# Padded bin rows, and one plain loop in place of staggered stages, in a Fourier filter with routed experts

## The chip, the core and the metric

The kernel runs on one core of one Trainium2 chip. The metric is device time in microseconds, the median of several runs. The engines are called PE (TensorE), DVE (VectorE), ACT (ScalarE), POOL (GpSimd) and SP (SyncE); PE, DVE, ACT and POOL compute, and SP only issues DMAs here.

## The reference

What is computed, cut to what matters (B = 8 batches, S = 2496 positions, D = 256 columns, N = B S = 19968 rows, E = 8 experts of hidden size 1024):

```python
X = np.fft.rfft(x, axis=1)
Y = X * (filt_r + 1j * filt_i)[None]
y = np.fft.irfft(Y, n=S, axis=1).reshape(N, D)

logits = y @ w_gate + modality_bias[modality_id]
e_idx = np.argmax(logits, axis=1)
gate_w = softmax(logits)[arange(N), e_idx]
for e in range(E):
    mask = e_idx == e
    h = np.maximum(y[mask] @ w1[e], 0.0)
    out[mask] = gate_w[mask, None] * (h @ w2[e])
```

## The kernel before

The Fourier transform of length 2496 = 48 x 52 is done as products with small matrices, in three stages per batch, all in 16-bit floats with sums in PSUM.

- **Stage one** (`stage1`, 13 pieces a batch): products of `w1m` with pieces of x (L222); ACT copies each piece to `t1` (L225), and SP writes every second one to the DRAM buffer `b1_d` (L228).
- **Stage two** (`stage2`, 12 pieces and one step behind): `t2` is read back from `b1_d` in three chunks (L415); products with `w2m` (L431), ACT copies to `xf` (L443), DVE multiplies with the filters `g1` and `g2` (L445, L446), products with `a1m` and `a2m` (L438, L439), ACT copies to `z` (L452), and SP writes to `b2_d` (L454).
- **Stage three** (`stage3`, 10 pieces and two steps behind): `t4` is read from `b2_d` in four chunks (L422); products with `wbm` (L477, L478), scaled into `yo` by ACT or DVE by turns; a step later the rows are transposed on PE (L489) and copied to `yT` by DVE (L498); another step later they are multiplied with the gate weights (L494), and DVE adds the logits (L507).
- **Routing** (`count`, `place`, `table`): the expert of each row, its place in the expert's bin, and the blocks of 256 rows that are full. `scatter` writes the rows of `yo` to the bins in DRAM with indirect DMAs from POOL (L561). A row of a bin holds 256 halves, the row's number and its gate weight: RW = 130 words, 520 bytes.
- **Experts** (`Experts.step`): a block of a bin is loaded by SP (L635), turned by PE (L661), multiplied with the first matrix (L672), passed through relu by ACT (L676), multiplied with the second (L684), scaled by DVE (L691) and scattered to the output by POOL (L694). There are 85 blocks, four steps each. Up to three blocks are loaded ahead.

The tiles of `t2` and `t4` come from one pool of three buffers (`bp`, tag `t24`), and the PSUM tiles of the three stages, of the transposes `lt` and of `place` from another of three (`pp`, tag `ps`). A new tile waits until the one three allocations earlier has been read.

Ahead of the loop the matrices are made: POOL writes index patterns, DVE makes phases of them, ACT takes the sine (`turns_to_cos`, L190). Stage one of batch 0 is written between `w1m` and the larger `w2m`. `a1m` and `a2m` are `w2m` and a changed copy `w2x` of it, turned by products with a permutation (L309), evicted by DVE and ACT. Half of each filter tile is read from DRAM, and the other half is copied within SBUF (L258, L259).

One loop then runs over steps n. Batch g is offset by `GAP` = 14 steps from the batch before it; its stage two starts at 14 g + 16 and its stage three at 14 g + 32; `load_t2` and `load_t4` are asked `LEAD` = 2 steps ahead; `count` comes 12 steps after the start of stage three and `place` one later. Each step also runs 2.25 expert steps (`STEPS`), and the weights of one expert are asked on every fourth step from the first on. What is left of the experts follows the loop. The framework orders the instructions of each engine from this program: an engine works through its own instructions in order, and so do the DMA queues of SP and POOL.

Of the kernel before, what the change touches and what calls it, by code (L numbers as in the profile page):

```python
# [20 lines left out]
P = 128  # L21
# [7 lines left out]
def kernel(  # L29
# [47 lines left out]
    RW = DW + 2  # L77
# [11 lines left out]

    RND = float(3 << 22)  # L90
    TWO_PI = 2.0 * math.pi

    zbias = const_pool.tile([P, 1], F32)
    nc.vector.memset(zbias, 0.0)
# [20 lines left out]

# [13 lines left out]
    pp = ctx.enter_context(tc.tile_pool(name="fpsum", bufs=3, space=bass.MemoryType.PSUM))  # L129
    hp = ctx.enter_context(tc.tile_pool(name="hpsum", bufs=2, space=bass.MemoryType.PSUM))  # L130
    op = ctx.enter_context(tc.tile_pool(name="opsum", bufs=1, space=bass.MemoryType.PSUM))
# [18 lines left out]
    gen = tc.alloc_tile_pool(name="gen", bufs=1)  # L150
    k1_i = gen.tile([KA, 2, NS], I, name="k1_i")
    nc.gpsimd.iota(k1_i, pattern=[[0, 2], [1, NS]], base=0, channel_multiplier=0)
    for _ in range(3):
        load_x()
    k2_i = gen.tile([KB, NS, N2], I, name="k2_i")
    nc.gpsimd.iota(k2_i, pattern=[[1, NS], [N1, N2]], base=0, channel_multiplier=0)
    nc.gpsimd.iota(k2_i[:, :, H:N2], pattern=[[1, NS], [-N1, H]], base=N1 * (N2 - 1), channel_multiplier=0)
    nc.gpsimd.iota(k2_i[:, 0, :], pattern=[[N1 // 2, 2], [N1, H]], base=0, channel_multiplier=0)


    wg_f = const_pool.tile([P, DC, E], F32)
    nc.sync.dma_start(wg_f, moe_w_gate.rearrange("(a p) e -> p a e", p=P))
    mb_sb = const_pool.tile([1, n_mod * E], F32)
    nc.sync.dma_start(mb_sb, moe_modality_bias.rearrange("a e -> (a e)")[None, :])
    mid_h = dataclasses.replace(moe_modality_id.tensor, shape=list(moe_modality_id.tensor.shape))
    mid32 = mid_h.ap().bitcast(I32).rearrange("(g p w) -> p g w", g=B, p=KA)
    mraw = gen.tile([P, B, 2 * NTT], I32, name="mraw")
    nc.sync.dma_start(mraw[:KA], mid32)
    mrawc = gen.tile([P, 3, B, 2 * NTT], I32, name="mrawc")
    for b in range(3):  # L170
        nc.sync.dma_start(mrawc[KA:P, b], mid32[b * KC:(b + 1) * KC])
    rows = row_int([], rows_i, "rows")
    bit0 = row_int([(ALU.bitwise_and, 1)], rows_i, "bit0")
    half = row_int([(ALU.arith_shift_right, 1)], rows_i, "half")
    def col(name, fn):
        t = fft_pool.tile([P, 1], F32, name=name)
        fn(t)
        return t
# [5 lines left out]
    nbit0 = col("nbit0", lambda t: ts(t, bit0, -1.0, 1.0))  # L184
    def turns_to_cos(dst, q, shape):

        r = gen.tile(shape, F32, tag="gen_r")
        ts(r, q, RND, RND, ALU.add, ALU.subtract)
        nc.vector.tensor_sub(q, q, r)
        nc.scalar.activation(dst, q, AF.Sin, bias=zbias[:shape[0], :], scale=TWO_PI)  # L190


    k1_f = gen.tile([KA, 2, NS], F32, name="k1_f")
# [13 lines left out]
    NP = NTT // EV  # L207
    NPY = NY // EV
    st = [dict() for _ in range(B)]

    def chunk_of(t):
        for c, (t0, t1) in enumerate(TCH):
            if t0 <= t < t1:
                return c, t0, t1

    def stage1(g, k):
        t = k * EV
        c, t0, t1 = chunk_of(t)
        xt = xts[g, c]
        ps = pp.tile([P, EV, D], F32, tag="ps")  # L220
        for i in range(EV):
            nc.tensor.matmul(ps[:KA, i, :], lhsT=w1m, rhs=xt[:, t - t0 + i, :], start=True, stop=True)  # L222
        if k % 2 == 0:
            st[g]["t1"] = rp.tile([KA, 2, EV, D], BF16, tag="t1", bufs=2, name="t1")
        nc.scalar.copy(st[g]["t1"][:, k % 2], ps[:KA])  # L225
        if k % 2 == 1 or k == NP - 1:
            n = (k % 2 + 1) * EV
            nc.sync.dma_start(b1_d[g, t + EV - n:t + EV].rearrange("t p c -> p t c"),  # L228
                              st[g]["t1"].rearrange("p a b d -> p (a b) d")[:, :n])

    def input_piece(g, k):

        stage1(g, k)
        if (k + 1) * EV in [t1 for t0, t1 in TCH]:
            load_x()

    ident = const_pool.tile([P, P], BF16)
    make_identity(nc, ident)

    Lexcl = const_pool.tile([P, P], F32)  # L240
    nc.gpsimd.memset(Lexcl, 0.0)
    nc.gpsimd.affine_select(
        out=Lexcl, in_=Lexcl, compare_op=ALU.is_ge, fill=1.0,
        base=0, pattern=[[-1, P]], channel_multiplier=1,
    )
    ones_sq = const_pool.tile([P, P], F32)
    nc.vector.memset(ones_sq, 1.0)


    for f_dram, g in ((filt_r, g1), (filt_i, g2)):  # L250
        by_c = f_dram[0:N1 * H, :].rearrange("(c s) d -> c s d", s=N1)
        rev = bass.AP(f_dram.tensor, f_dram.offset + (N1 - 1) * D,
                      [[N1 * D, H], [-D, NS - 1], [1, D]])
        nc.gpsimd.dma_start(g[0:H, 0:NS, :], by_c[:, 0:NS, :])
        nc.gpsimd.dma_start(g[H:N2, 1:NS, :], rev)
        nc.gpsimd.dma_start(g[H:N2, 0, :], by_c[:, NS, :])
        nc.gpsimd.dma_start(g[N2:N2 + 1, 0, :], f_dram[NF - 1:NF, :])
        nc.sync.dma_start(g[N2:KB, 1:NS, :], g[0:N2, 1:NS, :])  # L258
        nc.sync.dma_start(g[N2 + 1:KB, 0, :], g[1:N2, 0, :])  # L259

    for k in range(NP):
        input_piece(0, k)

    bit1 = row_int([(ALU.arith_shift_right, 1), (ALU.bitwise_and, 1)], rows_i, "bit1")
    quart = row_int([(ALU.arith_shift_right, 2)], rows_i, "quart")


    x_ro = col("x_ro", lambda t: nc.vector.tensor_single_scalar(t, rows, float(N2), op=ALU.is_ge))
    x_c = fft_pool.tile([P, 1], F32, name="x_c")
    nc.vector.scalar_tensor_tensor(x_c, in0=x_ro, scalar=-float(N2), in1=rows, op0=ALU.mult, op1=ALU.add)  # L270
    x_hi = col("x_hi", lambda t: nc.vector.tensor_single_scalar(t, x_c, float(H), op=ALU.is_ge))
    sgn = col("sgn", lambda t: ts(t, x_hi, -2.0, 1.0))
    x_c0 = col("x_c0", lambda t: nc.vector.tensor_single_scalar(t, x_c, 0.0, op=ALU.is_equal))
    wt0 = col("wt0", lambda t: ts(t, x_c0, -0.5, 1.0))

# [5 lines left out]
    ph1 = col("ph1", lambda t: ts(t, bit0, -0.25, 0.5))  # L281
    q2 = gen.tile([KB, NS, 2, N2], F32, name="q2")
    ts(q2[:, :, 0, :], k2_i, n2s[:KB], ph0[:KB])
    ts(q2[:, :, 1, :], k2_i, n2s[:KB], ph1[:KB])

    ts(q2[:, 0, 0, :], k2_i[:, 0, :], n2s[:KB], 0.25)
    ts(q2[:, 0, 1, :], k2_i[:, 0, :], n2s[:KB], 0.5)
# [6 lines left out]


# [9 lines left out]
    for s0 in range(0, NS, SPB):  # L305
        for src, dst in ((w2m, a1m), (w2x, a2m)):
            tp = pp.tile([P, EV * D], F32, tag="ps", name="tp")
            for i in range(SPB):
                nc.tensor.matmul(tp[:KB, i * KB:(i + 1) * KB], lhsT=src[:, s0 + i, :], rhs=perm,  # L309
                                 start=True, stop=True)  # L310
# [467 lines left out]
    while True:  # L778
# [3 lines left out]
        for g in range(B):  # L782
# [3 lines left out]
            if 0 <= k <= NS // EV:  # L786
                stage2(g, k)
# [63 lines left out]
```

## Time and profile before

| | |
|---|---|
| time, median of 3 runs | 876.86 us (872.82 to 879.74) |
| the profiled execution | 879.74 us |
| its span | 878.0 us |
| its mean granted PE clock | 0.811 |
| PE busy | 650.8 us (74%) |
| DVE, ACT, POOL busy | 385.7, 387.3, 367.7 us (44%, 44%, 42%) |
| DMA bytes | 106.80 MB |

The page gives the busy time of each engine, and the span in 40 slices of 22 us with the granted PE clock and the share of time that the 16 DMA engines were busy. Windows give the same for any stretch. A timeline lists instructions with their start, duration and, in brackets, the idle time of the engine ahead of them and what ended it. Starts of products on PE are times of issue, and their ends are modelled.

### The profile page before, as it was taken

The numbers are of one execution on the slowest core, as the hardware profiler recorded it, in microseconds if no ns is written. First come the engines' busy times: TensorE is split into PE (matmuls) and PEld (weight loads), VectorE is DVE, ScalarE is ACT, GpSimd is POOL, SyncE is SP. The second block draws the span as 40 slices with busy tenths as digits, with TensorE's granted clock in tenths as the row PEclk, the third lists the DMA queues.
The fourth block names the chain that finished last, engine by engine and source line by source line (L and its number), as shares of the span: only waits on it lengthen the run. The fifth ranks groups of instructions, "written<-read, shape, count | busy, mean of one in ns | idle before, by whom it ended". The sixth has DMA issues, their size and how long they took to land.

```text
span 878.0 us, 15948 instructions
## 1 busy us (share of the span) xinstructions
PE 650.8 (74%) x4886; PEld 497.7 (57%) x4886; DVE 385.7 (44%) x1248; ACT 387.3 (44%) x695; POOL 367.7 (42%) x413
## 2 busy tenths in 40 slices
PE   1463678697596787787956886877694679999996
PEld 1352446465365556565744674665473457777775
DVE  5431235346255434553733464454253224444442
ACT  1553335345254444463724543452242235555553
POOL 5131201625505433544345345435546544444444
PEclk9985555557579878897969899897897769999998
DMA  8799986566465446454533343342222223222320
GB/s 154 162 223 211 225 176 159 130 139 173 105 149 149 121 100 160 119 149 100 168 110 112 100 115 117 88 127 71 70 73 95 95 79 101 94 92 92 96 64 1
DMA packets 92696, 106.80 MB, mean 122 GB/s; under 512 B 12708, under 2 KB 75754, under 8 KB 92460
## 3 DMA queue, kind: packets, MB, share of 16 engines
q0 software_dynamic: 29120, 50.75, 24.8%
q1 hardware_dynamic: 63496, 55.03, 23.9%
q8 instruction: 44, 0.72, 0.4%
q14 instruction: 36, 0.29, 0.1%
HBM read 71.87 MB, written 54.31 MB: 144 GB/s over the span
## 4 chain that ended last, share of the span: by engine, by line
PE 23%; issue 17%; POOL 8%; another core or an unknown queue 4%; DMA 4%; DVE 3%; ACT 2%; POOLq 0%; SPq 0%; DVEq 0%; ACTq 0%
PE hps L672 7%; PE ops L684 6%; POOL out_dram L694 6%; DMA out_dram<-osb,meta 2%; PE ps L478 2%; POOL bins_d L561 2%; PE ps L477 2%; PE lt L489 1%; DMA bins_d<-yo,pos_i 1%; ACT hT L676 1%; PE ps L431 1%; PE pT L661 1%; PE pz L439 1%; PE pz L438 1%
## 5 line engine op out<-in xcount | busy, mean ns | idle before, releaser
L676 ACT ACTIVATE hT<-hps 128x512 f16<-128x512 f32 x340 | 197.4, 597 | 282.1 <-PE hps L672 131.6
L694 POOL DMA_INDIRECT out_dram<-osb,meta x170 | 168.1, 989 | 269.0 <-DVE osb L691 220.3
L672 PE MATMUL hps<-xT,w 128*128 128x256 f16 x1360 | 231.4, 293 | 32.8 <-ACT hT L676 16.5
L684 PE MATMUL ops<-w2sb,hT 128*128 x1360 | 226.6, 289 | 9.8 <-issue 9.3
L561 POOL DMA_INDIRECT bins_d<-yo,pos_i x160 | 156.7, 979 | 58.3 <-issue 47.3
L684 PEld LDWEIGHTS <-hT 128*128 128x128 f16 x1360 | 141.2, 104 | 45.2 <-issue 18.4
L672 PEld LDWEIGHTS <-w 128*128 128x128 f16 x1360 | 131.9, 104 | 61.2 <-issue 24.8
L225 ACT CAST t<-ps 96x512 f16<-96x512 f32 x104 | 59.7, 583 | 92.5 <-PE ps L222 31.6
L651 DVE COPY w<-w1sb 128x2048 f16 x85 | 59.2, 697 | 63.4 <-PE ops L684 46.7
L477 PE MATMUL ps<-t,wbm 96*96 96x256 f16 x160 | 56.8, 355 | 40.4 <-ACT t L225 18.8
L662 DVE COPY xT<-pT 128x512 f16<-128x512 f16 x85 | 35.9, 423 | 112.2 <-remote 39.9
L445 DVE TENSOR_TENSOR p<-xf,g 104x512 f16<-104x512 f16 x96 | 40.6, 423 | 96.4 <-ACT xf L443 80.3
L691 DVE TENSOR_SCALAR osb<-ops,meta 128x256 f32<-128x256 f32 x170 | 74.9, 477 | 15.6 <-PE ops L684 9.4
L222 PE MATMUL ps<-xt,w1m 96*96 96x256 f16 x208 | 53.3, 358 | 36.0 <-DVE w1m L205 16.7
L125 POOL DMA_DIRECT2D xt<-in_x_dram x32 | 18.9, 590 | 143.4 <-PE ps L222 117.4
L431 PE MATMUL ps<-t,w2m 104*104 104x256 f16 x192 | 48.4, 344 | 40.4 <-issue 12.0
L498 DVE COPY yT<-lt 128x512 f16<-128x512 f16 x80 | 33.8, 422 | 94.2 <-remote 43.5
L438 PE MATMUL pz<-p,a1m 104*104 104x256 f16 x192 | 62.4, 338 | 16.1 <-ACT t L225 5.9
L452 ACT CAST z<-pz 104x512 f16<-104x512 f32 x96 | 56.7, 590 | 34.5 <-PE pz L439 9.5
L443 ACT CAST xf<-ps 104x512 f16<-104x512 f32 x96 | 56.4, 587 | 23.2 <-PE ps L431 15.5
L439 PE MATMUL pz<-xf,a2m 104*104 104x256 f16 x192 | 62.9, 341 | 1.3 <-DVE xf L446 1.1
L489 PE MATMUL lt<-ident,yo 128*128 128x128 f16 x320 | 40.2, 264 | 24.4 <-ACT xf L443 16.6
(185 smaller groups left out, 632.1 us busy)
## 6 DMA issues: line engine op xcount, KB each, us to landing
xs<-bins_d SPq DMA_DIRECT2D x85, 130.0 KB
t<-b_d SPq DMA_DIRECT2D x24, 416.0 KB
b_d<-z SPq DMA_DIRECT2D x48, 208.0 KB
xt<-in_x_dram POOLq DMA_DIRECT2D x24, 384.0 KB
b_d<-t SPq DMA_DIRECT2D x48, 192.0 KB
t<-b_d SPq DMA_DIRECT2D x24, 384.0 KB
w1sb<-in_moe_w_dram POOLq DMA_DIRECT2D x8, 512.0 KB
w2sb<-in_moe_w_dram POOLq DMA_DIRECT2D x8, 512.0 KB
```

Source lines behind the costliest of these rows:

```text
L225: nc.scalar.copy(st[g]["t1"][:, k % 2], ps[:KA])
L431: nc.tensor.matmul(ps[:KB, i, :], lhsT=w2m[:, s + i, :], rhs=st[g]["t2", s // SCH][:, s % SCH + i, :], start=True, stop=True)
L438: nc.tensor.matmul(pz[:KB, i, :], lhsT=a1m[:, s_ + i, :], rhs=p1[:, i, :], start=True, stop=False)
L439: nc.tensor.matmul(pz[:KB, i, :], lhsT=a2m[:, s_ + i, :], rhs=p2[:, i, :], start=False, stop=True)
L477: nc.tensor.matmul(ps[:KA, i, :], lhsT=wbm, rhs=t4[:, t - t0, :], start=True, stop=True)
L561: ins = nc.gpsimd.indirect_dma_start(out=bins_d[:, :], out_offset=IOA(ap=st[g]["pos"][:rows, t:t + 1], axis=0), in_=st[g]["yw"][:rows, t, ...
L651: cp = nc.vector.tensor_copy(b["w1"].rearrange("p a f -> p (a f)"), w1sb[:, ds(ej, 1)].rearrange("p o a f -> p (o a f)"))
L672: mm = nc.tensor.matmul(hps[:, k, :], lhsT=b["w1"][:, dc, ft * P:(ft + 1) * P], rhs=b["xT"][:, dc].rearrange("p i t -> p (i t)"), start=(d ...
L676: nc.scalar.activation(b["hT"][:, q * FQ:(q + 1) * FQ, :], hps, AF.Relu)
L684: nc.tensor.matmul(b["ops"][:, i, :], lhsT=b["hT"][:, ft, i * P:(i + 1) * P], rhs=w2sb[:, ds(b["ej"], 1), ft, :], start=(ft == 0 and i == ...
L691: nc.vector.tensor_scalar_mul(osb[:, i, :], b["ops"][:, i, :], gate[:, i, :])
L694: ins = nc.gpsimd.indirect_dma_start(out=out[:, :], out_offset=IOA(ap=b["meta"][:, i, 0:1], axis=0), in_=osb[:, i, :], in_offset=None, **kw)
```

## The change

The rows of the bins grow from 130 to 144 words (520 to 576 bytes); POOL sets the 14 added words of each row to zero. With that the rest of the program takes another form:

- The matrices are all made ahead of stage one. `a1m` and `a2m` are turned by PE transposes with the identity, eight to a PSUM tile, and evicted by DVE in permuted order. The column index `k2_i` is copied to floats first.
- Both halves of each filter tile are read from DRAM.
- The modality ids are read after the matrices, and the three parts for the last 32 partitions go one after the other through one tile.
- The loop runs over i and k: stage one of batch i, stage two of batch i-1 and stage three of batch i-2, at the same k (0 to 13). `t2` and `t4` are loaded where they are first used.
- In stage three the transposes, their copy, the products with the gate weights and the sum of the logits belong to one step; `count` and `place` are one function, `route`, at k = 11.
- The weights of the experts are asked in i = 2 and 3.

```diff
-    RW = DW + 2
+    RW = DW + 16
...
-    for s0 in range(0, NS, SPB):
-        for src, dst in ((w2m, a1m), (w2x, a2m)):
-            tp = pp.tile([P, EV * D], F32, tag="ps", name="tp")
-            for i in range(SPB):
-                nc.tensor.matmul(tp[:KB, i * KB:(i + 1) * KB], lhsT=src[:, s0 + i, :], rhs=perm,
-                                 start=True, stop=True)
-            ev = nc.vector.tensor_copy if dst is a1m else nc.scalar.copy
-            ev(dst[:, s0:s0 + SPB, :].rearrange("p s c -> p (s c)"), tp[:KB, 0:SPB * KB])
+    SPB = 8
+    with tc.tile_pool(name="turn_psum", bufs=2, space=bass.MemoryType.PSUM) as tpp:
+        for src, dst in ((w2m, a1m), (w2x, a2m)):
+            for s0 in range(0, NS, SPB):
+                tp = tpp.tile([KB, SPB, P], BF16, tag="tp")
+                for i in range(SPB):
+                    nc.tensor.transpose(tp[:, i, :KB], src[:, s0 + i, :], ident[:KB, :KB])
+                nc.vector.tensor_copy(
+                    dst[:, s0:s0 + SPB, :].rearrange("p s (jr t) -> p s t jr", jr=4),
+                    tp[:, :, :KB].rearrange("p s (t jr) -> p s t jr", jr=4))
...
-        nc.sync.dma_start(g[N2:KB, 1:NS, :], g[0:N2, 1:NS, :])
-        nc.sync.dma_start(g[N2 + 1:KB, 0, :], g[1:N2, 0, :])
+        for ro in range(2):
+            p0 = ro * N2
+            nc.gpsimd.dma_start(g[p0:p0 + H, 1:NS, :], by_c[:, 1:NS, :])
+            nc.gpsimd.dma_start(g[p0 + H:p0 + N2, 1:NS, :], rev)
...
+        for b in range(3):
+            nc.sync.dma_start(mraw[KA:P], mid32[b * KC:(b + 1) * KC])
+            nc.vector.tensor_copy(mids[KA:P, :, b:NYF:3], mv[KA:P, :, 3:4 * NYG:4, 0])
...
         if s < NS:
+            if s % SCH == 0:
+                src = b1_d[g].rearrange("t (jr s) c -> (t jr) s c", jr=4)
+                st[g]["t2"] = bp.tile([KB, SCH, D], BF16, tag="t24", name="t2")
+                nc.sync.dma_start(st[g]["t2"], src[:, s:s + SCH, :])
...
+            nc.gpsimd.memset(yw[:, :, DW + 2:RW], 0)
...
-        if k > 1:
-            yT = st[g]["yT"]
+            yT = sp.tile([P, EV, DC, P], BF16, tag="yT", bufs=2)
+            nc.vector.tensor_copy(yT, pT)
             for i in range(EV):
                 for dc in range(DC):
                     nc.tensor.matmul(psL[:, i, :], lhsT=yT[:, i, dc, :], rhs=wg[:, dc, :],
...
-    GAP = NP + 1
-    OFF2 = NP + 3
-    OFF3 = OFF2 + NS // EV + 1 + 3
-    LEAD = 2
...
+    for i in range(B + 4):
+        for k in range(NP + 1):
+            if i < B and k < NP:
+                stage1(i, k)
+                if (k + 1) * EV in [t1 for t0, t1 in TCH]:
+                    load_x()
+            if 0 <= i - 1 < B and k <= NS // EV:
+                stage2(i - 1, k)
+            if 0 <= i - 2 < B and k <= NPY:
+                stage3(i - 2, k)
...
+            if 0 <= i - 2 < B and k == NPY + 1:
+                route(i - 2)
+                tabs[i - 2] = table(KR[i - 2], i - 2 == B - 1)
+                to_bins.append([i - 2, 0])
+            if 2 <= i < 4 and k % 3 == 0 and k // 3 < 4:
+                load_w((i - 2) * 4 + k // 3)
```

`t4` is loaded in the same way as `t2`, at every third k of stage three.

## The prediction

> **What bounds the kernel now.** I read the totals and slices of the page first, then windows by stage, then the timelines of the engines at the start, and last the chain that ended last.
>
> ```profile
> span 878.0 us, 15948 instructions
> ...
> PE   1463678697596787787956886877694679999996
> ...
> PEclk9985555557579878897969899897897769999998
> DMA  8799986566465446454533343342222223222320
> ```
>
> PE is the busiest engine, but over different limits. Three stretches show in the windows:
>
> ```profile
> 100.00:140.00 40.00, 34.15 (x170) 22.16 (x170) 14.43 (x38) 16.78 (x30) 1.57 (x3) 0.50 0.92 185
> 250.00:700.00 450.00, 337.28 (x2704) 258.04 (x2703) 211.34 (x710) 197.10 (x358) 208.38 (x219) 0.86 0.42 114
> 750.00:850.00 100.00, 94.99 (x851) 78.48 (x850) 48.01 (x118) 54.17 (x95) 45.88 (x47) 1.00 0.29 93
> ```
>
> (Columns: busy time of PE, weight loads, DVE, ACT, POOL, then granted clock, DMA share, GB/s.) Up to 120 us the DMA engines are full (share 0.9 to 1.2) and PE runs at half clock; from 250 to 700 stages and experts share PE, 75% busy; from about 707 only experts are left, one block per 4.25 us, bound by PE. The start, from the timelines of DVE, ACT and PE:
>
> ```profile
> 16.37 0.23 DVE L205 TENSOR_SCALAR w1m<-w,bit 96x48 f16<-96x48 f16 x1
> 20.43 2.76 DVE L189 TENSOR_TENSOR q<-q,r 104x2496 f32<-104x2496 f32 x1
> 30.11 2.38 ACT L190 ACTIVATE w2m<-q,zbias 104x2496 f16<-104x2496 f32 x1
> 46.15 0.67 PE L431 MATMUL ps<-t,w2m 104*104 104x256 f16 x2 [5.18 <-DMA t<-b_d]
> 92.00 0.67 PE L431 MATMUL ps<-t,w2m 104*104 104x256 f16 x2 [6.66 <-DMA t<-b_d]
> 100.13 0.45 PE L477 MATMUL ps<-t,wbm 96*96 96x256 f16 x1 [2.53 <-DMA t<-b_d]
> ```
>
> w1m is ready at 16.6 and stage one runs from 16.7, but stage two waits for its input until 46.15, and again at 92.0: what counts is when a batch has been written to DRAM and read back, not when stage one began. The stage-three starts (first L477 of each batch) are 100, 151, 207, 271, 357, 436, 520 and 595 us: 51, 55 and 64 us per batch while there are no experts, then 86, 79, 84, 75.
>
> Inside the middle stretch PE stands still for 2 to 7 us at a time, much of it ahead of stage three:
>
> ```profile
> 322.96 0.27 PE L477 MATMUL ps<-t,wbm 96*96 96x256 f16 x1 [4.33 <-ACT t L225]
> 366.12 0.37 PE L477 MATMUL ps<-t,wbm 96*96 96x256 f16 x1 [4.86 <-issue]
> 469.97 0.27 PE L477 MATMUL ps<-t,wbm 96*96 96x256 f16 x1 [4.14 <-ACT t L225]
> ```
>
> **The change, part by part.** *Work and order.* Both built programs have the same 4869 products on PE, and 42 of the 85 expert blocks stand behind the last stage product in both (42.25 before). The tail of 42 x 4.25 us is unchanged, so what remains is the time to reach it.
>
> *The start.* Removed: stage one ahead of the big matrices; x loads 4 to 7 early; the two SBUF copies of the filters. Added: 8 filter loads more from DRAM, transposes with identity evicted by DVE, an int-to-float copy, and the modality loads, three of them one after the other. DVE loses its wait for the modality data (idle 5.28 us ahead of 12.71) and ACT does not stop for stage-one writes ahead of w2m (9.33 us of DVE idle at 32.52). Sum: POOL has the last iota at about 7.5 us (its rows, 1.8 for the loads, 1.3 and 0.75 for iotas); DVE then 0.9 copy + 1.8 + 0.5 + 1.5 + 2.8 = 15; ACT 2.4; fix 0.6; PE starts turning at about 19. Six DVE evictions of 832 elements a row: xT's row (512 f16 in 0.42) gives 0.69 each, two of L312 (416 f32 in 0.59) give 1.18; behind w2x (0.9), PE is done at 24 to 27, I take 26. Stage one therefore starts 9 us later than 16.7. It now runs without ACT blocked behind w2m: seven writes of b1 through two buffers, each a pair of copies (1.05) and a landing (2.3 to 2.9 us in this trace before DMA saturates), one every 1.8 us, the last issued about 38.5, with the modality loads between them on SP. It lands at 41, and the t2 load (4.3 us at 41.8 in the trace) at 45.5 to 46.5. Before: 46.15. I take 0; bounds -4 (weights leave POOL at about 40 instead of 45.3) and +10 (filters cost 26 x 23 x 2 packets of 512 B at 60 ns over 16 engines, 4.5 us, and 3.5 for the long rows, less 4.9 for the copies; the modality chain at 10 us a load, as in the saturated trace, would hold SP's writes).
>
> *Stages without offsets.* Stage two of a batch now begins one iteration after its last stage-one piece instead of three, stage three likewise; loads are no longer asked two iterations ahead, though buffers still let most go early. From the trace, issue to last byte between 120 and 700 us: b1 write 3.3 median (2.4 to 4.5 quartiles), t2 load 4.45 (4.2 to 5.2), b2 write 2.5, t4 load 3.5. After the last stage-one product: ACT 0.58 plus one instruction ahead of it, 1.2; 3.3; 4.45: 8.9 us. In the built order 50 products of 256 columns and four transposes lie between; the tail prices a product at 0.106, at clock 0.86 that is 6.5 us. PE, in order, stands 2.4 us, and 0.6 more for t4, whose chain (1.7 + 2.5 + 3.5, and behind t2 on SP) ends later: 3 us. SP holds the expert loads and the b1 and b2 writes behind the t2 wait, but three expert blocks are loaded ahead. Five such boundaries: 15 us. Bounds: 0 (half clock: 50 x 0.213 = 10.7 covers) and 7.6 each (upper quartiles plus an expert load of 2.1 on SP). Before, these spacings were 11 to 22 us, above 8.9, so nothing is saved. The three boundaries without experts are bare in both: 11.7 less 2 of PE work is 9.7, and the old waits there were 6.66 + 2.53, 6.65, 4.30 + 3.72 and several of 1 to 3; with 14 iterations of 3.56 us I get 152 and 206 for the next stage-three starts against 151 and 207. I take +2 (-4 to +10).
>
> *Logits in the same step.* lt is now held over transposes, the DVE copy and the logits. DVE 0.42 plus 0.1 to 0.2 of signals; the built order puts 4 products (0.85 at half clock) or about 8 (0.85 to 1.0) between. Covered when DVE is free; +3 in all. If the copy always stands behind another DVE instruction of 0.42 to 0.70, 1.3 per step: 0.45 x 30 + 0.4 x 50 = 33. One placement step instead of two: the same DVE chain; 0.
>
> *Padding.* Scatter packets of 8 rows take 191 ns, expert reads (1040 B) 47 ns median; by bytes (x1.108) that is 3 and 5 us of all 16 engines over 500 us at a share of 0.2 to 0.5: hidden, since an expert load lands in 2.1 us and three lie ahead; uncovered, 0.2 us per block, 17. Were aligned rows as cheap as the 4096 B output packets (180 ns), 2 us saved, hidden too. Eight POOL memsets: at most 0.5 each (128x128 f32 took 0.20), ahead of L463, on an engine idle 58%. I take 0.
>
> [...]
>
> [...]
>
> *Sum:* 0 + 2 + 15 + 3 + 0 = +20. The profiled execution took 879.7 us (span 878.0 and 1.7 around it), the median of the runs is 876.9: 897 on the median.
>
> **The rivals.** *Faster, by the ring of loads.* t2 and t4 share three buffers. Before, the third t4 chunk takes the buffer that stage two frees one iteration ahead of its use; after, one freed three iterations ahead. If the six L477 gaps of the middle (3.64 + 3.48 + 4.33 + 4.86 + 4.14 + 4.33 = 25) are that load, they go, and if the boundaries cost 1 us or less, 877 + 2 + 3 + 5 - 25 = 862. It decides once a boundary costs under 2 us. For: five of these gaps fall past the first chunk. Against: two name ACT, and t4 loads land in 3.5 us, less than an iteration. *Much slower, by the logits:* the 33 us in place of 3: 927. For: DVE is 47% busy in that stretch; against: the built order moved expert products in between. *No change:* boundaries covered at half clock and all else hidden: 880. For: by the sums above before and after meet within 2 us at 46, 100, 151 and 207; against: PE is at full clock in most expert-only stretches. The padding as such may do nothing measurable in any of these.
>
> **How the numbers follow.** Forecast (slower by 10 to 38 us) 0.48; much slower 0.15; no change 0.19; faster 0.18. The likeliest is 897, its own range 885 to 915; taking in the faster case's 862 and the slower case's 927 gives 860 to 930. About 1% is what a measurement of this kernel can tell from no change. Faster by over 1%: 0.17; within: 0.18; slower: 0.65.
>
> **What would show it.** Stage one first at about 26 us, stage two at 46, stage three at 96 to 100, 152, 206 (start right); then about 4 us more per batch, with PE idle ahead of stage two at each batch's start, released by t<-b_d (boundaries right); idle ahead of the logits (L479) under 10 us in all; the tail again 42 blocks of 4.25 us. Wrong, if stage two first starts after 56 us, if the middle shrinks, or if the padded reads become the releaser of the experts' turns.

## The result, and the profile after

| | before | after |
|---|---|---|
| median | 875.1 us (4 runs, 872.82 to 879.74) | 945.3 us (4 runs, 940.57 to 951.52) |
| ratio, 95% interval | | 1.0799 [1.0707, 1.0891] |
| span of the profiled execution | 878.0 us | 939.5 us |
| PE busy | 650.8 us | 657.9 us |
| DMA bytes | 106.80 MB | 109.27 MB |

The change costs 70 us; 20 were forecast, and 945 lies outside the range of 860 to 930. PE does 7 us more work by its modelled ends. The rest is waiting, and most of it is early, as the slices of the page after show (one slice is 23.5 us here):

```profile
span 939.5 us, 15952 instructions
...
PE   0316369459469677877866885788478459999996
...
DMA  9299974644734744564573434334222322333320
```

The second DMA slice is a 2: from 23 to 47 us hardly anything moves (33 GB/s, a share of 0.21). What DVE does then, from its timeline:

```profile
19.95 7.50 DVE L273 COPY a1m<-tp 104x832 f16<-104x832 f16 x2
27.09 4.04 DVE L273 COPY a1m<-tp 104x832 f16<-104x832 f16 x1
30.76 11.39 DVE L273 COPY a2m<-tp 104x832 f16<-104x832 f16 x3
41.77 0.39 DVE L276 TENSOR_SCALAR a1m<-a1m,wt 104x104 f16<-104x104 f16 x1
```

The six evictions with which `a1m` and `a2m` are turned take 3.75, 3.75, 4.04 and three times 3.80 us. They hold DVE from 20 to 42 us, and the first products of stage one, which follow the turning on PE, wait until they are done. PE's timeline (the number ahead of the engine is the busy time, the bracket the idle time ahead of it):

```profile
42.20 0.60 PE L331 MATMUL mb_ps<-mb_sb,ones_sq 1*128 1x16 f32 x2 [6.49 <-DVE a1m L276]
43.07 3.30 PE L393 MATMUL ps<-xt,w1m 96*96 96x256 f16 x14 [0.27 <-DVE bias_b L332]
...
71.98 0.67 PE L412 MATMUL ps<-t,w2m 104*104 104x256 f16 x2 [16.11 <-DMA t<-b_d]
...
124.49 0.67 PE L412 MATMUL ps<-t,w2m 104*104 104x256 f16 x2 [18.21 <-DMA t<-b_d]
126.59 0.45 PE L464 MATMUL ps<-t,wbm 96*96 96x256 f16 x1 [1.43 <-DMA t<-b_d]
...
182.19 0.67 PE L412 MATMUL ps<-t,w2m 104*104 104x256 f16 x2 [8.58 <-DMA t<-b_d]
...
252.16 0.67 PE L412 MATMUL ps<-t,w2m 104*104 104x256 f16 x2 [10.04 <-DMA t<-b_d]
```

Stage one starts at 43.07 in place of 16.7, stage two at 71.98 in place of 46.15. Then each batch's stage two waits for the batch to come back from DRAM: 18.2, 8.6 and 10.0 us for the next three. The windows show what goes on during the longest of these waits, and that the pace of the tail is as before (95.0 us of PE in 100):

```profile
100.00:126.00 26.00, 5.74 (x22) 3.74 (x21) 1.89 (x5) 5.36 (x11) 3.56 (x5) 1.00 1.17 213
...
800.00:900.00 100.00, 95.09 (x852) 78.60 (x850) 47.99 (x120) 54.07 (x96) 46.35 (x48) 1.00 0.30 96
```

From 100 to 126 us PE is busy for 5.74 us while the DMA engines are full (share 1.17): beside x and the stages' own transfers they carry the expert weights, which POOL began to ask for at 55.6 us and of which 15 of 16 pieces have landed by 129. The last three writes of `b1` land 11.6, 13.0 and 9.3 us after their issue there, and the `t2` load behind them takes 6.9. The groups of PE's products that lost most (busy, mean ns, idle ahead, releasers):

```profile
L412 PE MATMUL ps<-t,w2m 104*104 104x256 f16 x192 | 49.0, 347 | 79.7 <-DMA t<-b_d 66.5 <-ACT xf L424 7.8 <-DVE yo L486 5.4
...
L479 PE MATMUL lt<-wg,yT 128*128 128x8 f16 x320 | 21.5, 173 | 18.2 <-DVE yT L476 10.2 <-issue 4.3 <-DVE yo L486 2.9
L512 PE MATMUL psO<-c,Lexcl 128*128 128x8 f32 x16 | 3.2, 272 | 9.9 <-DVE c L510 7.6 <-ACT hT L651 1.6 <-DVE xT L637 0.6
```

The same three before:

```profile
L431 PE MATMUL ps<-t,w2m 104*104 104x256 f16 x192 | 48.4, 344 | 40.4 <-issue 12.0 <-DMA t<-b_d 11.8 <-ACT t L225 7.2
...
L494 PE MATMUL lt<-wg,yT 128*128 128x8 f16 x320 | 21.3, 172 | 7.4 <-DVE yT L498 7.1 <-issue 0.4
L537 PE MATMUL psO<-c,Lexcl 128*128 128x8 f32 x16 | 3.2, 274 | 3.5 <-DVE c L528 1.9 <-DVE xT L662 0.9 <-issue 0.6
```

The starts of stage three cut the two executions into four stretches that can be set against the terms of the prediction:

| stretch | before | after | difference | forecast |
|---|---|---|---|---|
| 0 to stage three of batch 0 | 100.1 | 126.6 | +26.5 | 0 |
| on to stage three of batch 3 (first expert blocks only) | 170.5 | 199.1 | +28.6 | +2 |
| on to stage three of batch 7 (with experts) | 324.2 | 329.8 | +5.6 | +15 |
| on to the end | 283.2 | 284.0 | +0.8 | 0 |

(The forecast's +3 for the logits has no stretch of its own.) Of the first +26.5, 25.8 are there when stage two of batch 0 starts. From there to stage three of batch 0 the two take 54.0 and 54.6 us, both with the DMA engines full, so the longest wait, the 18.2 us in that stretch, adds next to nothing:

```profile
46.15:100.13 53.98, 27.45 (x116) 21.83 (x116) 12.76 (x30) 23.13 (x44) 14.89 (x20) 0.60 1.17 214
```

```profile
71.98:126.59 54.61, 24.67 (x100) 18.68 (x100) 10.89 (x26) 19.93 (x38) 10.12 (x15) 1.00 1.17 210
```

The mean granted clocks of the two profiles (0.811 and 0.883) can't be set against each other: the clock's record begins at 54 us in one trace and at 232 us in the other, and the time ahead of it counts as 1.00. From 126 to 163 us in the trace after, products of 256 columns are typically issued 0.213 us apart, as in the trace before at a recorded 0.50 (0.109 in the tail of both, at 1.00). The kernel before ran in 858.6 us at a mean clock of 0.895 and in 858.6 at 0.826, on one chip, so that mean tells nothing of the time.

Two things are needed to read the numbers below. The experiments ran on other chips than the result, of two kinds: some run the kernel before in 754 to 756 us, some in 866 to 872, so an experiment is told by its ratio to the kernel before on its own chip, with that kernel's time, and times of one chip are not set against another's. Only the first 150 us are the same on all (stage three of batch 0 at 99.8 to 101.0 and of batch 1 at 149.3 to 152.5 in the traces of five kernels that share that part), and there times are compared directly. And some runs were disturbed: e5 and e6 were left with too few for an interval and were repeated as e15 and e14, and of e16's profile only the start is read. Expectations in microseconds assume the chip of the result (875.1 us before); they are compared as ratios.

### The profile page after: what moved, and what is told of

It reads as the page before. It is cut to its first block, busy times and chain, and to the rows that moved or that the text cites. A ratio compares the mean times of both kernels' runs of the same rounds, so it can differ in the third digit from the quotient of the medians.

```text
span 939.5 us, 15952 instructions
## 1 busy us (share of the span) xinstructions
PE 657.9 (70%) x4886; PEld 492.1 (52%) x4886; DVE 411.7 (44%) x1249; ACT 385.2 (41%) x689; POOL 381.0 (41%) x431
## 2 busy tenths in 40 slices
DMA packets 94346, 109.27 MB, mean 116 GB/s; under 512 B 13162, under 2 KB 77456, under 8 KB 94162
## 4 chain that ended last, share of the span: by engine, by line
PE 37%; issue 20%; DMA 13%; POOL 8%; DVE 8%; another core or an unknown queue 7%; ACT 5%; SPq 0%; POOLq 0%; ACTq 0%; DVEq 0%
PE hps L647 8%; PE ops L659 7%; DMA b_d<-t 6%; POOL out_dram L669 6%; PE ps L465 4%; PE ps L464 4%; DMA t<-b_d 4%; PE lt L474 3%; ACT t L396 3%; PE pz L420 2%; PE pz L419 2%; POOL bins_d L536 2%; PE ps L393 2%; PE ps L412 2%
## 5 line engine op out<-in xcount | busy, mean ns | idle before, releaser
L647 PE MATMUL hps<-xT,w 128*128 128x256 f16 x1360 | 233.2, 291 | 34.9 <-ACT hT L651 17.1
L659 PE MATMUL ops<-w2sb,hT 128*128 x1360 | 229.9, 288 | 11.1 <-issue 10.0
L536 POOL DMA_INDIRECT bins_d<-yo,pos_i x160 | 157.4, 984 | 50.9 <-issue 48.3
L647 PEld LDWEIGHTS <-w 128*128 128x128 f16 x1360 | 131.4, 103 | 60.9 <-issue 33.5
L659 PEld LDWEIGHTS <-hT 128*128 128x128 f16 x1360 | 138.7, 103 | 46.1 <-issue 20.1
L464 PE MATMUL ps<-t,wbm 96*96 96x256 f16 x160 | 58.4, 365 | 32.8 <-ACT t L396 19.6
L424 ACT CAST xf<-ps 104x512 f16<-104x512 f32 x96 | 56.2, 587 | 49.4 <-PE ps L412 39.3
L412 PEld LDWEIGHTS <-w2m 104*104 104x104 f16 x192 | 29.7, 164 | 85.7 <-DMA t<-b_d 55.5
L393 PE MATMUL ps<-xt,w1m 96*96 96x256 f16 x208 | 53.2, 354 | 16.6 <-ACT t L396 12.1
```

Source lines behind the costliest of these rows:

```text
L412: nc.tensor.matmul(ps[:KB, i, :], lhsT=w2m[:, s + i, :], rhs=st[g]["t2"][:, s % SCH + i, :], start=True, stop=True)
L464: nc.tensor.matmul(ps[:KA, i, :], lhsT=wbm, rhs=t4[:, t - t0, :], start=True, stop=True)
L536: ins = nc.gpsimd.indirect_dma_start(out=bins_d[:, :], out_offset=IOA(ap=st[g]["pos"][:rows, t:t + 1], axis=0), in_=st[g]["yw"][:rows, t, ...
L647: mm = nc.tensor.matmul(hps[:, k, :], lhsT=b["w1"][:, dc, ft * P:(ft + 1) * P], rhs=b["xT"][:, dc].rearrange("p i t -> p (i t)"), start=(d ...
L659: nc.tensor.matmul(b["ops"][:, i, :], lhsT=b["hT"][:, ft, i * P:(i + 1) * P], rhs=w2sb[:, ds(b["ej"], 1), ft, :], start=(ft == 0 and i == ...
```

## The experiments

The theories: (1) the start costs what it does by the evictions' price, and by the loads and writes that meet the weights; (2) the loop costs by the slack taken out between the stages, and the logits and the routing in one step add to it. Rivals: the padding, the missing lead of the loads, or one of start and loop alone.

**e1, the padding alone.**

```diff
-    RW = DW + 2
+    RW = DW + 16
...
+            nc.gpsimd.memset(yw[:, :, DW + 2:RW], 0)
```

> The kernel before with rows of the bins of 576 bytes and the zeroing on POOL, and nothing else of the change. If the padding costs nothing (the trace after has scattered writes of 2.42 us from issue to landing beside 2.25, reads of a block of 2.19 beside 2.09): 871 to 880 us. If the wider rows cost what eight rows per 4.25 us of a block or the scatters can cost: up to 17 us more, 892 us. If rows that are a multiple of 64 bytes travel faster: under 866.

Measured: 0.9998 [0.9956, 1.0039], before 755.6. Rows of 576 bytes in place of 520 are worth nothing that can be measured, either way. The groups that read them, in e1 and in e10 below (520 bytes, a chip of the same kind), wait for their blocks:

```profile
L658 DVE COPY meta<-xs 128x4 int32<-128x4 int32 x85 | 15.7, 185 | 127.9 <-DMA xs<-bins_d 111.7 <-DMA out_dram<-osb,meta 13.7 <-DVE osb L692 1.2
```

```profile
L657 DVE COPY meta<-xs 128x4 int32<-128x4 int32 x85 | 15.0, 179 | 135.0 <-DMA xs<-bins_d 122.0 <-DMA out_dram<-osb,meta 10.7 <-DVE osb L691 0.8
```

111.7 us with the padding, 122.0 without (and with the routing in one step): no sign that wider rows come later.

**e3, the new start with the old loop; e2 and e11, the old start with the new loop** (rows of 520 bytes in all three; e11 is e2 again).

```diff
 # e3, in the kernel after
-    for i in range(B + 4):
-        for k in range(NP + 1):
+    for k in range(NP):
+        input_piece(0, k)
+    GAP = NP + 1
+    OFF2 = NP + 3
...
 # e2 and e11, in the kernel before
-    OFF2 = NP + 3
...
+    for i in range(B + 4):
+        for k in range(NP + 1):
+            if 0 < i < B and k < NP:
```

> The start of the kernel after (everything made first, transposes with permuted evictions, loads of the modality bits late) with the stage functions, the offsets, the loads ahead and the loop of the kernel before; rows of 520 bytes. Theory 1: stage two of batch 0 at 70 to 74 us and then the pace of before, 900 to 908 us. Rival, the old loop's slack takes up part of a late start: 880 to 895. Rival, the start is the whole loss: 940.

> The start of the kernel before (batch 0's stage one while the matrices are made, turning by products) with the stage functions, the route and the plain loop of the kernel after; rows of 520 bytes. Theory 1, start and loop cost independently and the loop's bare boundaries cost some 29 us in the batches without experts and 6 later: 905 to 915 us, with stage two of batch 0 at 46 to 50 us and waits for t2 of 8 to 18 us at the next two or three batches. Rival, the loop costs little by itself and the late start pushes everything that follows: 875 to 890. Rival, the loop is the whole loss: 940.

> The same kernel as e2, beside the parts of its loop on one chip. If the parts add up (bare boundaries 1.014, logits in the same step 1.011, the route in one step as e10 says): 1.03 to 1.04 on a chip that runs the kernel before in 865 to 875 us, 1.05 to 1.06 on one that runs it in 755. If they are one loss counted several times: 1.015 to 1.02.

Measured: e3 1.0326 [1.0245, 1.0407], 779.0 beside 755.6; e2 1.0573 [1.0477, 1.0668], 799.7 beside 755.6; e11 1.0503 [1.0384, 1.0621], 794.2 beside 754.1. Both halves cost. e3 came as theory 1 had it (900 to 908 us, 1.028 to 1.038); e2 cost more than that theory said (905 to 915 us, 1.034 to 1.046). The old loop's slack takes up little of a late start: stage three of batch 0 comes at 128.0 us in e3, 27 us late, and the end is 23 us later. The loop is the larger half, 40 to 44 us. In e11 PE's idle time stands where the kernel after has it:

```profile
L422 PE MATMUL ps<-t,w2m 104*104 104x256 f16 x192 | 48.6, 345 | 61.2 <-DMA t<-b_d 61.2
...
L488 PE MATMUL lt<-wg,yT 128*128 128x8 f16 x320 | 21.1, 172 | 22.0 <-DVE yT L485 21.3
...
L521 PE MATMUL psO<-c,Lexcl 128*128 128x8 f32 x16 | 3.1, 268 | 8.2 <-DVE c L519 8.2
```

The same three groups in e1, which has the old loop:

```profile
L431 PE MATMUL ps<-t,w2m 104*104 104x256 f16 x192 | 47.6, 339 | 15.0 <-DMA t<-b_d 12.7 <-ACT t L225 2.2
...
L495 PE MATMUL lt<-wg,yT 128*128 128x8 f16 x320 | 21.1, 172 | 10.1 <-DVE yT L499 10.1
...
L538 PE MATMUL psO<-c,Lexcl 128*128 128x8 f32 x16 | 3.2, 274 | 3.8 <-DVE c L529 3.6 <-ACT t L225 0.2
```

Waiting for `t2` grows by 48 us, for `yT` by 11, for `c` by 5; waiting for `t4` falls by 10, from 13.3 us to 3.5. The sum of 54 is more than the 34 us between the two spans (789.5 and 755.5), since some of it takes the place of other idle time.

**e5 and e15, the kernel after again**, on two other chips.

> The kernel after, unchanged, beside the other three, since the chip of the first four experiments ran the kernel before in 755 us and not in 875. If start and loop are all of the change and add up there (e2 costs 44 us, e3 23): 815 to 830 us where the kernel before takes 755, a ratio of 1.08 to 1.10. If the two overlap: 800 to 812.

> The kernel after, unchanged. If the start (e3, 1.033) and the loop (e2 and e11, 1.057 and 1.050) add up: 1.08 to 1.09 of the kernel before on a 755 us chip; 1.07 to 1.08 on an 866 us chip.

Measured: e5 930.0 us beside 865.7 (no interval); e15 1.0899 [1.0824, 1.0974], 947.5 beside 872.3. The sum of e3 and e11, 8.3%, stands beside 8.0% for the result and 9.0% for e15, so start and loop add up roughly, as far as chips of two kinds can be compared (for the slower kind 1.07 to 1.08 was expected of e15). On a 755 us chip the kernel after was not run.

**e16, the permuted evictions alone**, in the kernel before, at the old place in the start.

```diff
-    SPB = 4
+    SPB = 8
...
-            ev(dst[:, s0:s0 + SPB, :].rearrange("p s c -> p (s c)"), tp[:KB, 0:SPB * KB])
+            nc.vector.tensor_copy(
+                dst[:, s0:s0 + SPB, :].rearrange("p s (jr t) -> p s t jr", jr=4),
+                tp[:KB, :, :KB].rearrange("p s (t jr) -> p s t jr", jr=4))
```

> The kernel before with the two matrices turned by transposes, eight to a tile, and evicted by DVE with the permuted write of the kernel after, at the old place (from 34 us on, stage one of batch 0 long done). If the eviction's 3.7 us are the instruction's own: six of them hold DVE from 34 to 57 us, the first product with a1m waits from 48 to 57, stage three of batch 0 begins at 108 to 113 in place of 100, ratio 1.008 to 1.016. If they were long in the kernel after only because loads by POOL ran beside them there: 0.6 to 1.2 us each and a ratio under 1.003.

Measured: 1.0194 [1.011, 1.0278], 891.2 beside 872.3. DVE's timeline of e16:

```profile
34.37 11.18 DVE L308 COPY a1m<-tp 104x832 f16<-104x832 f16 x3
45.17 11.40 DVE L308 COPY a2m<-tp 104x832 f16<-104x832 f16 x3
```

3.73 and 3.80 us each, with POOL idle from 29 to 59 us. The price is the instruction's own and not that of POOL's loads beside it. Stage two begins at 57.0 and stage three at 112.5 us, as expected; the ratio is a little over the 1.008 to 1.016.

**e4, the kernel after, turned by products; e17, the kernel after, with the permutation on the reading side.**

```diff
 # e4: the kernel before's turning
+                    nc.tensor.matmul(tp[:KB, i * KB:(i + 1) * KB], lhsT=src[:, s0 + i, :], rhs=perm, ...)
+                ev = nc.vector.tensor_copy if dst is a1m else nc.scalar.copy
 # e17: the same elements in the order of the destination
-                    dst[:, s0:s0 + SPB, :].rearrange("p s (jr t) -> p s t jr", jr=4),
-                    tp[:, :, :KB].rearrange("p s (t jr) -> p s t jr", jr=4))
+                    dst[:, s0:s0 + SPB, :].rearrange("p s (jr t) -> p s jr t", jr=4),
+                    tp[:, :, :KB].rearrange("p s (t jr) -> p s jr t", jr=4))
```

> The kernel after, with the two matrices turned by products with a permuted unit matrix, four to a PSUM tile in float32, and evicted in order by DVE and ACT, as before; all else as after. Theory 1, the six permuted evictions of 3.7 us (22 us of DVE) hold the start: stage one begins at 25 to 30 us in place of 43, and the time falls by 8 to 20 us, to 925 to 937. Rival, the late input loads and POOL's order hold the start anyway (the wait for the last b1 writes behind the weights): the time falls by less than 5 us, 940 to 946.

> The kernel after with the six evictions walking their tiles in the order of the destination: the writes to SBUF are contiguous, and the permutation lies in the reads of PSUM (steps of 8 bytes). If it is the strided write of 2 bytes (52 bytes apart, four to a row) that makes an element cost 4.5 ns: 0.7 to 1.2 us each in place of 3.7, stage one of batch 0 from 27 to 29 us on in place of 43, stage two from 55 to 58, the time 10 to 16 us below the kernel after's (ratio to the kernel before 1.06 to 1.075). If any permuted order costs it: 3.5 to 4 us each and 1.08 to 1.09.

Measured: e4 1.0763 [1.0671, 1.0854], 808.7 beside 755.6; e17 1.0636 [1.0564, 1.0707], 806.7 beside 755.7. e17 differs from the kernel after in the order of the copies alone; in e4 ACT also takes half of the evictions. DVE and PE in e17:

```profile
20.43 1.97 DVE L273 COPY a1m<-tp 104x832 f16<-104x832 f16 x2
...
23.34 3.00 DVE L273 COPY a2m<-tp 104x832 f16<-104x832 f16 x3
```

```profile
57.00 0.67 PE L412 MATMUL ps<-t,w2m 104*104 104x256 f16 x2 [16.72 <-DMA t<-b_d]
```

One swap of two letters on each side of a copy takes it from 3.75 to 1.0 us. In both kernels stage one begins 14 to 16 us earlier than in the kernel after (28.6 and 27.3), and stage two at 57.0 in place of 72.0. So the dear order is the one that writes halves 52 bytes apart in SBUF, at 4.5 ns an element (3750 / 832), against 1.2 for reads of PSUM in steps of 8 bytes. The two orders also differ in the length of the innermost run, 4 elements against 26, and no run separates the two. The gain at the start is shown by the traces; that it reaches the end in full is not: e17 came out as expected, but the ratio of e4 lies within the kernel after's interval and in the range of e4's rival (940 to 946 us, 1.074 to 1.081).

**e12, e4 with the weights held back** until POOL's eighth load of x.

```diff
-                load_w((i - 2) * 4 + k // 3)
+                with tc.issue_after(x_ins[7]):
+                    load_w((i - 2) * 4 + k // 3)
```

> e4 (the kernel after, matrices turned by products) with POOL's loads of the expert weights held behind its eighth load of x, which waits for stage one of batch 1. In e4 stage one ended at 37.9 us and stage two began at 57.0, with the last b1 writes landing after 5.7 and 7.8 us and the first t2 load after 7.0. If the weights on the DMA engines are what stretches these: landings of 2 to 3 us and of 4 to 5, stage two of batch 0 at 47 to 50 us, and the end 7 to 10 us earlier than e4's. If they stay as long: stage two at 55 to 58.

Measured: 1.055 [1.0443, 1.0657], 801.9 beside 754.1. The window from 40 to 58 us and PE's start of stage two, first of e4, then of e12:

```profile
40.00:58.00 18.00, 1.63 (x7) 1.18 (x7) 4.02 (x11) 2.48 (x5) 5.85 (x6) 1.00 1.17 218
```

```profile
56.95 0.67 PE L415 MATMUL ps<-t,w2m 104*104 104x256 f16 x2 [15.33 <-DMA t<-b_d]
```

```profile
40.00:58.00 18.00, 4.89 (x21) 4.03 (x22) 5.07 (x15) 5.21 (x10) 1.03 (x4) 1.00 0.73 165
```

```profile
53.38 0.67 PE L417 MATMUL ps<-t,w2m 104*104 104x256 f16 x2 [10.47 <-DMA t<-b_d]
```

The DMA share falls from 1.17 to 0.73, the `t2` load takes 4.4 us in place of 7.0, and stage two starts 3.6 us earlier although stage one started 1.1 later. The last two writes of `b1` stay long (5.7 and 5.5 us): the weights are part of the collision, not all of it, and the forecast of 47 to 50 us was missed. The end comes 5 us earlier by the medians where 7 to 10 were expected. At the next boundary nothing is won: stage two of batch 1 starts 21 us after stage one has ended (83.7 to 105.0 us), with the weights now there.

**e6 and e14, the slack taken out of the kernel before; e7, the lead; e9, both.**

```diff
 # e6, e14 and e9
-    OFF2 = NP + 3
-    OFF3 = OFF2 + NS // EV + 1 + 3
+    OFF2 = NP + 1
+    OFF3 = OFF2 + NS // EV + 2
...
-    n = NP
+    n = NP - 1
 # e7 and e9
-    LEAD = 2
+    LEAD = 0
```

> The kernel before with the slack between the stages taken out (stage two 14 steps behind stage one in place of 16, stage three 14 behind stage two in place of 16), loads still issued two steps ahead. Theory 2, the bare boundary is what the loop costs (write to DRAM, landing, load, landing: about 3 + 4 us, of which nothing lies behind other work when there are no experts): 6 to 10 us at each of the first three or four batches and some us later, 30 to 45 us in all, ratio 1.04 to 1.06. Rival, issuing the load in the step that reads it is the cost: ratio under 1.015 here.

> The same kernel as e6 (slack out, lead kept). e9, with the lead out as well, cost 1.0305 on a chip that runs the kernel before in 754 us; e6 cost 1.014 on one that takes 866. If the lead is worth nothing and the chips differ: 1.025 to 1.035 on a 755 us chip. If the lead is worth half of e9's loss: 1.012 to 1.018 there.

> The kernel before with its slack kept and every t2 and t4 load issued in the step that first reads it (no steps ahead). Theory 2: with two spare steps the b1 write has long landed, so the load alone is in the way, 4 us less what the experts hide, at seven loads a batch (a buffer ahead is no longer filled): ratio 1.02 to 1.05. Rival, the queue of SP runs ahead by itself, since a load waits only for its buffer and its source: ratio under 1.01.

> The kernel before with both the slack (e6) and the two steps of lead (e7) taken out. e6 alone cost 1.014 and e7 alone nothing. Theory 2, with bare boundaries the first load can't go earlier than the last write, so the lead is worth nothing there either: 1.010 to 1.018, as e6. Rival, the lead covers the later loads of a batch once the boundary is late: 1.025 to 1.04.

Measured: e7 1.0005 [0.996, 1.0051], 864.5 beside 865.7: with the slack in place, asking the loads two steps ahead is worth nothing, against my theory's 1.02 to 1.05. e14 1.0151 [1.0097, 1.0205], 885.0 beside 872.3 (e6: 878.1 beside 865.7), against my theory's 1.04 to 1.06; e9 1.0305 [1.022, 1.0389], 775.3 beside 754.1, against 1.010 to 1.018. Ahead of stage two, e14 and then e9, with e9's placement:

```profile
L431 PE MATMUL ps<-t,w2m 104*104 104x256 f16 x192 | 49.2, 349 | 57.6 <-DMA t<-b_d 51.2 <-issue 6.4
```

```profile
L431 PE MATMUL ps<-t,w2m 104*104 104x256 f16 x192 | 48.7, 346 | 59.6 <-DMA t<-b_d 55.4 <-DVE yo L504 4.1
...
L537 PE MATMUL psO<-c,Lexcl 128*128 128x8 f32 x16 | 3.1, 263 | 8.0 <-DVE c L528 8.0
```

Two offsets alone make nearly the whole of the wait for `t2` (61.2 in e11), and of the wait for `c` (8.2 in e11) too. Whether e9's larger ratio is the lead, as its rival had it (1.025 to 1.04), or the kind of chip stays open, as no chip ran both. The like idle times ahead of stage two speak for the chip, and so do the stretches: from stage three of batch 0 to that of batch 3, e9 takes 11.9 us more than e1 and e14 12.1 more than the kernel before; on to batch 7, e9 takes 3.1 more and e14 7.2 less.

**e8, logits in the same step; e10, counting and placing in one step**, each alone in the kernel before.

```diff
 # e8
-        if k > 1:
-            yT = st[g]["yT"]
+            yT = sp.tile([P, EV, DC, P], BF16, tag="yT", bufs=2)
+            nc.vector.tensor_copy(yT, pT)
 # e10
-            if k == NPY + 3:
                 place(g)
```

> The kernel before with each pair's logits made in the step of its turning (products behind the DVE copy yT), offsets and loads as before. If PE's wait for that copy costs what it measured in the trace after (1.5 to 3.6 us in some steps, nothing in most): 5 to 12 us, ratio 1.007 to 1.016. If it is hidden by the steps' other work: ratio under 1.005. If it costs in each of 80 steps: 33 us, ratio 1.04.

> The kernel before with the counting and the placing of a batch in one step, so that PE's products with the counts (psO) stand right behind DVE's chain to c. The trace after has waits of 2.5 us there at 171 and 241 us. If that is all, eight waits of at most 2.5 us: up to 20 us, taken as 8, ratio 1.005 to 1.015. If other work of the step hides it: under 1.005.

Measured: e8 1.011 [1.006, 1.0159], 876.1 beside 865.7; e10 1.0127 [1.0056, 1.0198], 764.6 beside 754.1. Both cost about 10 us, 80 logit steps together as much as 8 placements. The group of e8, then that of e10:

```profile
L492 PE MATMUL lt<-wg,yT 128*128 128x8 f16 x320 | 21.8, 174 | 25.9 <-DVE yT L489 20.1 <-issue 5.5
```

```profile
L537 PE MATMUL psO<-c,Lexcl 128*128 128x8 f32 x16 | 3.5, 289 | 11.1 <-DVE c L528 11.1
```

PE waits 0.25 us per step for `yT` (20.1 / 80) and 1.4 us per batch for `c` (11.1 / 8). With e9 the three parts of the loop make 5.4%, against 5.0 and 5.7 for the whole loop in e11 and e2, but they can't simply be added: e8 is from the slower kind of chip, and the wait for `c` is in e9 already. On one chip, e9 and e11 differ by the logits and the routing (and by where the weights are asked for): 1.0305 and 1.0503, some 15 us. The wait for `yT` goes from 3.3 to 21.3 us and that for `c` from 8.0 to 8.2, so nearly all of that is the logits, and placing in one step adds nothing that can be seen once the offsets are out.

**e13 and e18, three and four spare steps in the kernel before.**

```diff
-    OFF2 = NP + 3
-    OFF3 = OFF2 + NS // EV + 1 + 3
+    OFF2 = NP + 4
+    OFF3 = OFF2 + NS // EV + 1 + 4
 # e18: 5 in place of 4
```

> The kernel before with three spare steps between the stages in place of two. If a boundary still waits in the kernel before (its page has 12.7 us of PE's idle ahead of stage two and 13.3 ahead of stage three, ended by loads of t, in a trace of this kernel's pace): up to 10 us less, ratio 0.985 to 0.995. If two steps cover the write and the load already: 0.998 to 1.005, since each further step only puts off the experts.

> The kernel before with four spare steps between the stages; three gave 0.987. If the waits at the boundaries shrink further: 0.975 to 0.985. If three steps cover write and load already and each further step only puts off the experts: 0.985 to 0.995. If the ring of three t tiles is held longer and stalls the other stage's loads: over 0.995.

Measured: e13 0.987 [0.9831, 0.991], 859.8 beside 872.3; e18 0.9935 [0.9892, 0.9978], 751.4 beside 755.7. Both beat both kernels, by 1.3 and 0.6% for the kernel before; on chips of different kinds they can't be ranked. In e18 stage three hardly waits for its loads any more, stage two still does:

```profile
L477 PE MATMUL ps<-t,wbm 96*96 96x256 f16 x160 | 52.2, 326 | 3.9 <-ACT t L225 1.3 <-ACT xf L443 1.2 <-DMA t<-b_d 0.9
...
L431 PE MATMUL ps<-t,w2m 104*104 104x256 f16 x192 | 46.9, 332 | 20.1 <-DMA t<-b_d 14.8 <-ACT t L225 3.2 <-ACT z L452 0.7
```

(e1 had 13.3 and 12.7 us for `t<-b_d` there.) In e13 the waits for `t` are about what they were before (5.2 and 12.7 us ahead of stages three and two, 7.7 and 11.8 before); set against the trace of before, from a chip of the same kind, it is level up to 270 us and 16 us ahead at stage three of batch 7 (578.9 and 594.8), so the gain comes with the experts; what makes it was not settled.

## Why the prediction was wrong

**The start (forecast 0, measured +26.5)** failed in its first step: "xT's row (512 f16 in 0.42) gives 0.69 each, two of L312 (416 f32 in 0.59) give 1.18". Both rows are contiguous copies, and the added one writes in permuted order. The trace before held a nearer row, `perm` (L302), 104 halves copied in exactly that order:

```profile
16.52 0.40 DVE L302 COPY perm<-ident 104x104 f16<-104x104 f16 x1
```

It took nearly as long as 512 contiguous halves. At 3.8 ns an element it gives 3.2 us for 832, three to five times what I used; measured 3.75. PE was done turning at 36 and not at 26, the last eviction at 42, and stage one began 17 us after the forecast. Of the 26 us, e4 and e17 give back 15, and e12 another 3.6; the 7 us that are left at the start of stage two were not taken apart.

The same term failed a second time: it took the landing of `b1` at "2.3 to 2.9 us in this trace before DMA saturates" and the `t2` load at 4.3. The last two writes were issued at 55.7 and 56.2 us and took 8.5 and 8.9 us; the load behind them took 6.7. POOL had reached the weights by then:

```profile
51.75 4.91 SPq L399 DMA_DIRECT2D b_d<-t  x3
65.23 1.15 SPq L409 DMA_DIRECT2D t<-b_d  x3
```

I had seen that weights leave POOL earlier and counted it as a gain of up to 4. e12 shows 3.6 us as the weights' share in e4. "Wrong, if stage two first starts after 56 us" was the right alarm: it started at 72.

**The boundaries without experts (forecast +2, measured +28.6 with the logits, the routing and one expert block more in it).** The sum priced a boundary at 9.7 us (from 11.7, which it doesn't derive; its chain is 8.9) and set against it the old waits, as if the new ones took their place. The price was about right: 8.6 and 10.0 us at the two boundaries of this stretch that have no or few experts, and 4.75 at a third. What failed is the subtraction, for the old waits largely stayed:

```profile
100.13:270.62 170.49, 133.89 (x790) 93.21 (x791) 77.02 (x280) 79.47 (x144) 50.87 (x59) 0.59 0.67 154
```

```profile
126.59:325.73 199.14, 144.38 (x825) 99.44 (x825) 83.64 (x296) 81.57 (x146) 59.29 (x69) 0.83 0.53 124
```

PE's idle time went from 36.6 to 54.8 us. What loads of `t` end grew from 5.2 to 26.0 us and what `c` ends from 1.1 to 5.8; all the rest shrank by 7 us only, from 30 to 23. The other 10.5 us are busy time, with 76 products of L647 in place of 60 (an expert block has 16). e14 shows the wait alone: with the offsets taken out, that for `t2` goes to 51 us, 18.0 of it at the first boundary, in a stretch that is 2 us longer for it (56.2 and 54.0).

**The boundaries with experts (forecast +15, measured +5.6)** were sized well as waits: 3 us each were forecast, and stage two of batches 4 to 7 waited for `t2` for 4.75 (in the stretch above), 2.72, 3.85 and 1.31 us. But PE's idle time in this stretch did not grow, 77.4 us before and 76.2 after: on the chip of the result PE stood idle there for other reasons (below), and the new waits took the place of some of that. On a 755 us chip the same stretch is 268.5 us in e11 and 253.7 in e1, +14.8; that the kind of chip makes this difference was not tried by itself.

**The logits (forecast +3, bound 33)** were too cheap: e8 gives 1.1%, some 10 us, on the slower kind of chip, and e9 beside e11 some 15 on the faster; the idle time ahead of L479 was 18.2 us where under 10 was to show. **The placement (forecast 0: "the same DVE chain")** costs 1.3% by itself in e10: the chain is the same, but with a step between PE does other work meanwhile. With the offsets out, as in the kernel after, that work is missing with or without the step (8.0 us of waiting in e9, 7.6 after), so there the cost belongs to the offsets.

**The padding (forecast 0) and the tail (42 blocks, unchanged)** were right: e1 gives 0.9998, and the last stretch differs by 0.8 us. This is in part luck as to the tail, as that stretch holds one expert block less after (780 products of L647, 796 of L672 before) and should be some 4 us shorter; where they went was not traced. (One of its readings is off without changing the sum: both traces hold 4886 products, not 4869.)

**The rivals.** The faster one rested on gaps ahead of L477; idle time there fell only from 40.4 to 32.8 us, and no boundary fell under the 2 us from which it decides until the last of them. The much slower one came nearest with 927, by the wrong mechanism: it needed 0.4 us in each of 80 steps, where e8 has 0.25, and the logits are a seventh of the loss by e8.

## What to carry to other kernels

Price a copy from a row with the same order of writes, not the same number of elements; where an eviction from PSUM has to permute, try a contiguous write and a jumping read (3.75 to 1.0 us here). Empty steps between a write to DRAM and its reading are not waste: two of them were worth 1.5% on one kind of chip and, with the lead, 3% on the other, a third or fourth another 0.6 to 1.3%, while asking for the load earlier on top of them was worth nothing. A long wait is not a long loss: the longest here, 18.2 us, stood in a stretch that takes 54 us in both kernels, with the DMA engines full (share 1.17). And when a stage moves, look at what the DMA engines carry at its new time, and take landings from that stretch.

## What the runs showed of the hardware

- A DVE copy from PSUM that writes halves 52 bytes apart in SBUF, four to a run, took 4.5 ns an element; one that reads PSUM in steps of 8 bytes and writes in order 1.2; 512 contiguous halves from PSUM 0.42 us, 0.8 ns an element.
- With the DMA engines full (share 1.17), a write of `b1` to DRAM took 8 to 13 us to land between 73 and 126 us of the trace after, and 2.3 outside it (issued at 44.8, 48.3 and 129.3 us, where the share was 0.51 from 44 to 48, 0.86 from 48 to 51 and 0.28 from 126 to 134).
- Chips differ more than the change: the kernel before took 754 to 756 us on some and 866 to 875 on others. The first 150 us are the same. After that, on the slower kind, engines stand still for some us at a time (DVE once for 13.9), and the profile names no releaser but "issue" or "remote". From the longest waits of the kernel before on the chip of the result (us in all, times, longest):

```profile
PEld L478 <- issue: 64.4, 115, 5.3
ACT hT L676 <- remote: 60.2, 14, 8.1
...
DVE xT L662 <- remote: 39.9, 7, 13.9
```

  In e1, with the same stages on a 755 us chip, "issue" ends 29.3 us ahead of the first of these groups, at most 0.4 at a time, and "remote" is not among its longer waits. What it is was not found; no experiment was made on it.
